# Linear attention and a mixture of adapters on one core: an order given as tables, held stores, warming products, and a pair of batches

## The chip, the cores and the metric

The kernel runs on one core of one Trainium2 chip. TensorE multiplies matrices, VectorE, ScalarE and GpSimd work element by element, SyncE only issues transfers; each takes its instructions in the order in which they were written. The metric is device time in microseconds, from the first instruction to the last landed transfer.

## The reference

Two layers in a row, all in float32. Attention has 8 batches, 8 heads, 576 positions and head size 64; the mixture sees 4608 rows of 512.

```python
phi(x) = concat(relu(x) * cos(pi/2 * pos/S), relu(x) * sin(pi/2 * pos/S))   # 64 -> 128
kv  = einsum('bhsf,bhsd->bhfd', phi(k), v);  z = phi(k).sum(over s)
x   = einsum('bhsf,bhfd->bhsd', phi(q), kv) / (einsum('bhsf,bhf->bhs', phi(q), z) + 1e-6)
x   = x, heads side by side: [8*576, 512]
logits = x @ w_gate                       # 8 experts
top 2 of them, softmax of the two -> w
out = x + sum over the two e of w_e * ((x @ A[e]) @ B[e])      # A[e]: 512 x 16, B[e]: 16 x 512
```

## The kernel before

Positions are split as s = 9p + j, with 64 values of p on partitions and nine of j. GpSimd loads K, V and Q of each batch and turns them into bf16 on the way (`load`, L456): batches 0 and 1 in halves of four heads, the other six whole, 1.18 MB in float32 each. 

For each batch, `relu_k` (L464) takes the positive part of K, `vscale` (L474) multiplies V by the cosine and the sine, and `kv_mm` (L486) sums the products over j, 18 matrix products for four heads, in a PSUM tile `pnd`. `kv_evac` (L498) copies the result into a block matrix `BD`.

Then the 4608 rows go through in 36 groups of 128. A group is (b, x): for x below 4 it has the rows j = x and j = x + 4 of one batch, for x = 4 the rows j = 8 of two batches (`halves`, L542). Its steps: `qt` transposes Q (L556); ScalarE takes the positive part into `qTcs` (L561); VectorE makes the sine half from it with a table of tangents, `TT` (L573); `num` multiplies by BD (L586), 8 products of 128 rows, or 16 of 64 rows where a group has two batches, each with its own BD; `rden` and `xt` (L597, L602) divide by the denominator, which gives 128 rows of x in bf16; `xT` (L610) transposes them in four pieces of 128 columns, and ScalarE or VectorE copies the result out of PSUM (L616 and L618, the two lines of the helper `copy`).

Three groups at a time go through the mixture: `za` (L629) multiplies by `AW`, which holds A and the gate side by side; `max`, `mask`, `sig` and `zg` (L644 to L668) find the top two and weigh; `zgT` (L677) transposes; `dx` adds x (product with the identity, L688) and the adapters' output (product with `Ball`, L690); `osb` copies the sum to an output buffer; `store` (L698), on SyncE, sends it off. The last two of the 13 steps take two groups and one. A store of rows of one batch covers 64 partitions, one of two batches 128. There are three output buffers `OSB`, each for three groups.

A is loaded with d = 4p + i on partition p. Before use, 32 products with a selection matrix `S4` (L425), which GpSimd makes at the start with two instructions (L371, L372), turn A and the gate into pieces of 128 consecutive d.

Nothing of this order is in the loops. Every step is entered in a `Planner` with its engine or a choice of two, a duration, what it needs and makes, and which buffers it uses. `run` (L141) plays the steps through with these durations, takes at each moment the ready step with the smallest entry of the table `PLACES`, gives it the buffer that comes free first, and takes the engine from the table `CHOICE`. The steps are then emitted in the order of their planned starts.

Of the kernel before, what the change touches and what calls it, by code (L numbers as in the profile page):

```python
# [19 lines left out]
LATENCY = {"PE": 0.21, "DVE": 0.13, "ACT": 0.15, "POOL": 0.2, "SP": 0.0}  # L20
DMA_RATE = 0.41e6
DMA_LATENCY = 1.8
DMA_LANES = 8
WINDOW = 0.12


BLOCK, BLOCK_AT, FETCH, FETCH_IDLE = 256, 193, 6.0, 2.5
BEGIN = {"PE": 0.5, "DVE": 0.8, "ACT": 0.7, "POOL": 1.2, "SP": 0.5}

PLACES = [
    -123.82, -97.4, -47.96, -100.66, -30.1, -76.14, 1.18, -17.78, -44.16, -27.45, -102.04, -89.07, -92.75, -20.86,
    8.39, -106.17, -47.52, -51.4, -51.94, -15.2, -20.12, -30.7, -12.73, 41.89, 2.63, 50.86, -32.97, -71.21, -84.2,
    -45.08, -22.7, -44.06, -24.87, -129.18, -56.01, -83.44, -56.45, -23.35, -30.71, -50.56, -9.06, -37.34, -48.99,
    -117.74, 7.85, -46.8, -44.69, -23.35, -67.61, -1.25, -18.65, -42.11, -26.97, -17.26, -8.58, -36.25, -30.45, 61.59,
    31.91, -23.51, 7.81, -59.54, 48.23, -12.48, -11.74, -7.87, -7.7, -66.67, -34.33, -14.61, 22.04, 47.87, -20.83,
    43.94, -35.94, -5.83, 2.99, 18.68, 19.74, 69.59, 65.53, 15.31, -20.71, -7.31, 14.09, -19.09, 24.26, 3.28, 14.51,
    24.35, 40.94, 65.02, 49.01, 82.54, 68.11, 19.64, 70.84, 25.5, 20.21, 19.29, 24.87, 24.94, 64.18, 38.61, 24.78,
    29.61, -12.26, 47.16, 56.95, 48.54, 41.02, 52.02, 49.58, 114.82, 65.11, -7.37, 39.35, 56.79, 16.16, -28.22, 76.43,  # L40
    61.78, 96.28, 70.3, 62.17, 61.7, 83.83, -23.28, 64.9, 39.14, 78.88, 100.53, 74.28, 4.96, 11.73, -67.43, -28.8,
    -34.01, -44.78, -13.42, -65.51, -7.6, 9.03, 21.45, -29.56, -32, -3.44, -20.48, -23.62, -45.49, -61.04, 29, -27.8,
    -17.72, -12.34, 17.18, -5.8, -41.41, -31.76, -12.71, 70.15, -43.08, -85.71, -51.88, 12.95, -31.28, 84.61, -11.54,
    27.95, -15.01, 26.35, 17.38, -4.76, -5.8, -10.36, -29.33, 61.17, 54.51, -2.53, 30.67, 31.34, -9.67, 43.39, 36.24,
    -11.07, 29.89, -28.3, 53.7, 14.2, -22.28, 85.34, 27, 43.28, -14.03, 12.63, -29.88, 26.57, -30.89, 71.13, 64.68,
    -34.05, 41.27, 26.54, 72.12, 38.76, 8.92, 82.64, 17.64, 52.18, 25.58, 1.08, 22.35, -23.14, -66.01, 63.23, 38.57,
    62.14, 23.07, 10.84, 10.98, -23.68, -7.79, 73.89, -37.19, 2.03, -25.04, 19.36, -22.76, 81.5, -23.57, 33.87, 1.89,
    -21.12, -6.03, 19.9, 16.84, -17.44, 14.66, 103.97, 43.62, -33.24, -3.64, -60.62, 62.32, 66.83, 31.16, 68.8, 39.32,
    39.39, 43.79, 52.34, 20.26, 18.55, 38.43, 67.49, 30.64, -19.72, 51.52, -0.52, 31.69, 18.56, 16.08, 32.31, 56.65,
    9.59, 5.09, 40.19, 25.14, 7.76, 72.6, 33.52, 61, 92.58, 20.72, 30.32, 26.33, -1.8, 7.33, 55.26, 53.91, 117.5,  # L50
    26.95, 32.11, 41.24, 51.61, -25.55, 64.34, 16.42, 7.19, 48.57, 34.95, 44.07, 1.01, 10.63, 44.37, 60.54, 12.46,
    32.58, 42.5, 22.25, 15.36, 63.52, 57.28, 20.55, 89.76, 61.89, -35.8, 52.54, 46.1, 40.19, 117.31, 78.88, 59.55,
    29.91, 39.68, 74.62, 33.38, 73.95, 64.93, 68.51, 58.86, 64.3, 79.01, 71.88, 29.75, 26.67, -5.07, 76.92, 9.96,
    72.4, 108.05, 80.33, 48.96, 100.43, -2.47, 62.93, 80.34, 79.57, -21, 59.04, 64.95, 88.66, 65.49, 83.05, 70.43,
    84.07, 57.5, 59.22, 53.56, 45.94, 61.36, 58.67, 64.22, 36.56, 76.22, 57.55, 66.06, 44.35, 117.26, 49.18, 63.07,
    93.92, 69.65, 79.94, 114.34, 45.23, 111.66, 68.79, 75.68, 72.53, 57.81, 47.97, 61.71, 28.28, 120.37, 66.4, 125.69,
    38.58, 91.77, 81.87, 82.14, 65.6, 40.48, 76.56, 78.09, 86.54, 114.37, 85.03, 27.38, 65.38, 40.32, 107.21, 137.42,
    83.89, 101.68, 83.47, 112.71, 91.66, 24.67, 115.02, 58.65, 121.01, 148.52, 55.54, 91.52, 82.4, 48.28, 109.21,
    64.04, 121.31, 47.23, 40.95, 99.89, 55.8, 28.32, 117.95, 23.61, 38.44, 138.24, 97.54, 52.55, 43.2, 16.05, 11.35,
    51.55, 37.09, -47.87, -15.39, -25.41, 28.01, 10.67, -15.69, 21.24, 7.06, -28.41, -20.59, 32.23, -44.3, -16.26,  # L60
    40.19, -16.58, -1.16, -20.84, -50.25, -15.22, -83.33, -46.78, 17.52, -45.48, -54.36, -34, -7.96, -20.96, -86.15,
    7.64, 0.67, 11.92, 77.19, 8.72, 3.46, -51.28, -33.12, -29.65, 50.9, -30.76, -27.31, -30.35, 79.56, -79.28, 8.86,
    -60.44, -52.39, 14.25, -53.52, -13.57, -2.65, -13.97, 21.28, 34.57, 25.69, 21.06, 47.19, 23.41, 20.77, -25.63,
    4.51, 51.34, 53.07, 69.07, 6.72, -12.58, 70.28, 6.9, -1.61, 36.02, 78.96, 63.2, 41.01, 132.03, -27.1, 99.32,
    -1.99, 15.68, 6.14, 20.32, 44.07, 10.98, -102.26, 31.86, 35.53, 75.79, 45.04, 39.6, 25.48, 50.85, 17.07, -16.97,
    9.89, 39.93, 33.37, 42.16, -8.97, -22.49, 32.6, 53.89, 30.65, 3.11, 70.8, 58.34, 21.93, 46.11, 104.63, 23.66,
    -32.61, 6.91, 53.06, -8.51, 73.15, -29.39, 88.37, 41.33, 53, 54.68, 58.28, 133.91, 76.33, 64.59, 23.33, -38.05,
    -14.23, 27.95, 34.17, 54.39, 56.91, 20.35, 63.26, 44.33, 37.33, 23.64, 45.07, 151.11, 93.72, 61.1, 117.26, 35.37,
    25.67, -9.73, 66.86, 97.88, 78.65, 125.31, 70.37, 87.58, 98.38, 66.86, 70.44, 87.69, 62.19, 45.01, 131.73, 8.97,
    56.76, 87.11, 110.15, 82.15, 79.31, 111.79, 87.29, 134.9, 107.5, 137.15, 31.17, 138.15, 46.56, 101.51, 85.3,  # L70
    56.94, 7.46, 25.9, 55.07, 88.7, 73.13, 128.67, 120.65, 47.61, 86.47, 110.69, 69.83, 58.53, 12.4, 93.33, 71.27,
    92.95, 31.16, 85.23, 85.5, 70.42, 95.75, 90.77, 90.1, 124.19, 130.22, 150.77, 134.12, 111.02, 111.53, 155.33,
    117.53,
]
CHOICE = [
    0, 0, 0, 0, 0, 0, 0, 0, 0, 0, 0, 0, 0, 0, 0, 0, 0, 0, 0, 0, 0, 0, 0, 0, 0, 0, 0, 0, 0, 0, 1, 0, 1, 0, 0, 0, 1, 0,
    0, 0, 1, 0, 0, 0, 1, 0, 0, 0, 1, 1, 0, 0, 0, 0, 0, 0, 0, 0, 1, 0, 0, 1, 0, 0, 0, 0, 0, 0, 0, 0, 0, 1, 0, 1, 0, 0,
    0, 0, 0, 0, 0, 0, 0, 0, 0, 0, 1, 0, 0, 0, 1, 0, 0, 0, 0, 1, 0, 0, 0, 0, 0, 0, 0, 0, 0, 0, 0, 0, 0, 0, 0, 0, 0, 0,
    0, 0, 0, 0, 0, 0, 0, 0, 0, 0, 0, 0, 0, 0, 0, 0, 1, 1, 0, 0, 1, 0, 0, 0, 0, 0, 0, 0, 1, 0, 0, 0, 0, 0, 0, 0, 0, 0,
    0, 0, 0, 0, 0, 0, 1, 0, 0, 0, 0, 0, 0, 0, 1, 0, 0, 0, 0, 0, 0, 0, 0, 0, 0, 0, 0, 0, 0, 0, 0, 0, 0, 0, 0, 0, 0, 0,  # L80
    1, 0, 0, 0, 0, 0, 0, 0, 0, 0, 0, 0, 0, 0, 0, 0, 0, 0, 0, 0, 0, 0, 0, 0, 0, 0, 0, 0, 0, 0, 0, 0, 0, 0, 0, 0, 0, 0,
    0, 0, 0, 0, 0, 0, 0, 0, 0, 0, 1, 0, 0, 0, 0, 0, 0, 0, 0, 0, 0, 0, 0, 0, 0, 0, 0, 0, 0, 0, 0, 0, 0, 0, 0, 0, 0, 0,
    0, 0, 0, 0, 0, 0, 0, 0, 0, 0, 0, 0, 0, 0, 0, 0, 0, 0, 0, 0, 0, 0, 0, 0, 0, 0, 0, 0, 1, 0, 0, 0, 0, 0, 0, 0, 0, 0,
    0, 0, 0, 0, 0, 0, 0, 0, 0, 0, 0, 0, 0, 0, 0, 0, 0, 0, 0, 0, 0, 0, 0, 0, 0, 0, 0, 0, 0, 0, 1, 0, 0, 0, 0, 0, 0, 0,
    0, 0, 0, 0, 0, 0, 0, 0, 1, 0, 0, 0, 0, 0, 0, 0, 0, 0, 0, 0, 0, 0, 0, 0, 0, 0, 0, 0, 0, 0, 0, 0, 0, 0, 0, 0, 0, 0,
    0, 0, 0, 0, 0, 0, 0, 0, 0, 0, 0, 0, 0, 0, 0, 0, 0, 0, 1, 0, 0, 0, 0, 0, 0, 0, 1, 0, 0, 0, 0, 0, 0, 0, 1, 0, 0, 0,
    0, 0, 0, 0, 1, 0, 0, 0, 0, 0, 0, 1, 0, 0, 0, 0, 0, 0, 0, 0, 0, 0, 0, 0, 0, 0, 0, 0, 0, 0, 0, 0, 0, 0, 0, 0, 0, 0,
    0, 0, 0, 0, 0, 0, 0, 0, 0, 0, 0, 0, 0, 0, 0, 0, 0, 0, 0, 0, 0, 1, 0, 0, 0, 0, 0, 0, 0, 0, 0, 0, 0, 0, 0, 0, 0, 0,
    0, 0, 0, 0, 0, 0, 0, 0, 0, 0, 0, 0, 0, 0, 0, 0, 0, 0, 0, 0, 0, 1, 0, 0, 0, 0, 0, 0, 0, 0, 0, 1, 0, 0, 0, 0, 0, 0,
    0, 0, 0, 0, 0, 0, 0, 0, 1, 0, 0, 0, 0, 0, 1, 0, 0, 0, 0, 0, 0, 0, 0, 0, 0, 0, 0, 0, 0, 0, 0, 0, 0, 0, 0, 0, 0, 0,  # L90
    0, 0, 0, 0, 0, 0, 0, 0, 0, 0, 0, 0, 0, 0, 0, 0, 0, 0, 0, 0, 0, 0, 0, 0, 0, 0, 0, 0, 0, 0, 0, 0, 0, 0, 0, 1, 0, 0,
    0, 0, 0, 0, 0, 0, 0, 0, 0, 0, 0, 0, 0, 0, 1, 0, 0, 1, 1, 0,
]

class Step:
    def __init__(self, idx, name, alts, due, needs, makes, uses, size, extra, ins):
# [713 lines left out]
```

## Time and profile before

Three runs took 124.2, 124.59 and 124.7 us; the median is 124.59. The profiled execution took 123.85 us, of which its records cover a span of 122.1.

| | busy us | share of the span | instructions |
|---|---|---|---|
| TensorE, products (PE) | 93.8 | 77% | 1328 |
| TensorE, weight loads (PEld) | 69.2 | 57% | 1328 |
| VectorE (DVE) | 98.3 | 81% | 280 |
| ScalarE (ACT) | 77.1 | 63% | 166 |
| GpSimd (POOL) | 28.7 | 24% | 43 |

The busy time of products is modelled: their pipelined ends overlap, so a busy TensorE isn't one at its peak. In the page's second part the span is cut into 40 slices of 3.05 us, and each digit is the busy share of a slice in tenths. In the groups a row reads: line, engine, operation, output <- input with shapes, count, then busy time and the mean of one in ns, then the idle time ahead of them and what ended it.

### The profile page before, as it was taken

How to read it: one execution, taken by the hardware profiler on the slowest of the kernel's cores; microseconds unless marked ns; L12 is line 12 of the kernel's file. 1: busy time of each engine (PE TensorE's matmuls, PEld its weight loads, DVE VectorE, ACT ScalarE, POOL GpSimd, SP SyncE). 2: the span in 40 equal slices, each digit the busy share in tenths (PEclk: the TensorE clock that was granted, in tenths of full speed). 3: DMA queues.
4: the chain of work that ended last, by engine and by line, in shares of the span. 5: the costliest groups of instructions: out<-in, count | busy, mean ns of one | idle time of the engine just before them, and what ended most of it. 6: DMA issues, size and time to landing. Idle time of an engine off the chain costs nothing.

```text
span 122.1 us, 3356 instructions
## 1 busy us (share of the span) xinstructions
PE 93.8 (77%) x1328; PEld 69.2 (57%) x1328; DVE 98.3 (81%) x280; ACT 77.1 (63%) x166; POOL 28.7 (24%) x43
## 2 busy tenths in 40 slices
PE   0007966999579779999799996999999999998100
PEld 0003745888357447877568765867766886662000
DVE  6431649988999999996999999999989999999100
ACT  5659669353693478686785974948194897567200
POOL 6995699922222222202002000000000000000000
PEclk9999996899999999999999999999999999999985
DMA  0999999999999999999999999998827660268791
GB/s 8 162 168 199 205 204 191 209 205 209 207 208 248 295 207 208 244 288 208 232 299 209 293 249 207 207 274 213 194 75 173 173 177 0 90 173 205 263 236 69
DMA packets 17246, 24.06 MB, mean 197 GB/s; under 512 B 2256, under 2 KB 14672, under 8 KB 17232
## 3 DMA queue, kind: packets, MB, share of 16 engines
q0 software_dynamic: 14096, 14.43, 71.2%
q1 hardware_dynamic: 3136, 9.44, 25.8%
q8 instruction: 10, 0.16, 0.5%
q14 instruction: 4, 0.03, 0.1%
HBM read 28.85 MB, written 9.44 MB: 314 GB/s over the span
## 4 chain that ended last, share of the span: by engine, by line
DMA 31%; DVE 28%; PE 24%; issue 5%; ACT 4%; POOL 2%; SPq 0%; DVEq 0%; POOLq 0%; ACTq 0%
DMA Kb<-in_k_dram 27%; PE pnd L492 9%; DVE xt L602 7%; DVE qTcs L573 5%; PE pnd L586 5%; DVE VV L483 4%; DMA out_dram<-osb 4%; PE ps L610 3%; DVE zg L668 2%; DVE BD L506 2%; DVE rden L597 2%; PE ps L629 2%; PE ps L688 2%; PE ps L690 1%; DVE m L644 1%
## 5 line engine op out<-in xcount | busy, mean ns | idle before, releaser
L586 PE MATMUL pnd<-BD,qTcs 128*128 128x130 bf16 (+1 forms) x320 | 23.9, 228 | 3.8 <-DVE xt L602 1.6
L483 DVE TENSOR_TENSOR VV<-Vb,TV 128x2304 bf16<-128x2304 bf16 (+1 forms) x18 | 20.5, 1149 | 6.3 <-DMA Vb<-in_v_dram 6.2
L602 DVE TENSOR_TENSOR xt<-pnd,rden 128x512 bf16<-128x512 f32 x36 | 24.2, 684 | 0.8
L586 PEld LDWEIGHTS <-qTcs 128*128 128x128 bf16 (+1 forms) x320 | 19.4, 103 | 7.7 <-issue 3.1
L561 ACT ACTIVATE qTcs<-ps 128x512 bf16<-128x512 bf16 x36 | 20.1, 601 | 3.1 <-PE ps L556 2.9
L492 PE MATMUL pnd<-VV,KR 64*128 64x260 bf16 x288 | 20.4, 287 | 0.8 <-DVE xt L602 0.5
L616 ACT COPY osb<-ps 128x512 f32<-128x512 f32 (+1 forms) x34 | 18.0, 569 | 4.3 <-DVE osb L618 2.0
L492 PEld LDWEIGHTS <-KR 64*128 64x128 bf16 x288 | 14.3, 99 | 5.1 <-issue 1.3
L616 ACT COPY xT<-ps 128x512 bf16<-128x512 bf16 x24 | 13.9, 588 | 4.8 <-PE ps L610 4.8
L573 DVE TENSOR_TENSOR qTcs<-qTcs,TT 128x512 bf16<-128x512 bf16 x36 | 15.3, 443 | 1.1 <-ACT qTcs L561 0.9
L610 PE MATMUL ps<-ident,xt 128*128 128x128 bf16 x144 | 13.4, 222 | 2.6 <-DVE xt L602 1.5
L690 PE MATMUL ps<-Ball,zgT 128*128 128x512 bf16 x36 | 13.5, 379 | 0.3 <-DVE zgT L618 0.3
L688 PE MATMUL ps<-xt,ident 128*128 128x512 bf16 x36 | 13.6, 379 | 0.0
L610 PEld LDWEIGHTS <-xt 128*128 128x128 bf16 x144 | 9.1, 99 | 6.7 <-DVE xt L602 3.2
L556 PE MATMUL ps<-ident,Qb 128*64 128x128 bf16 x288 | 11.9, 222 | 0.8 <-ACT qTcs L561 0.7
L504 ACT CAST BD<-pnd 64x260 bf16<-64x260 f32 x21 | 7.9, 378 | 5.2 <-PE pnd L492 3.9
L629 PE MATMUL ps<-AW,xT 128*128 128x136 bf16 x144 | 10.8, 223 | 0.4 <-ACT xT L616 0.2
L556 PEld LDWEIGHTS <-Qb 128*64 128x64 bf16 x288 | 8.9, 109 | 3.8 <-issue 2.4
L629 PEld LDWEIGHTS <-xT 128*128 128x128 bf16 x144 | 9.1, 98 | 2.4 <-DVE xT L618 0.6
L661 ACT ACTIVATE sig<-tt 128x24 f32<-128x24 f32 (+2 forms) x13 | 2.9, 222 | 11.2 <-DVE ps L654 6.1
L351 PE MATMUL ps<-tan_d,ones_f 64*128 64x512 f32 (+1 forms) x4 | 2.4, 751 | 9.5 <-DVE tan_d L343 9.5
L459 POOL DMA_DIRECT2D Qb<-in_q_dram x6 | 4.5, 751 | 17.3 <-PE ps L556 10.6
(55 smaller groups left out, 111.1 us busy)
## 6 DMA issues: line engine op xcount, KB each, us to landing
out_dram<-osb SPq DMA_DIRECT2D x20, 256.0 KB, 4.6
Kb<-in_k_dram POOLq DMA_DIRECT2D x6, 576.0 KB, 23.6
Vb<-in_v_dram POOLq DMA_DIRECT2D x6, 576.0 KB, 24.5
Qb<-in_q_dram POOLq DMA_DIRECT2D x6, 576.0 KB, 25.8
out_dram<-osb SPq DMA_DIRECT2D x8, 384.0 KB, 5.2
Kb<-in_k_dram POOLq DMA_DIRECT2D x4, 288.0 KB, 7.5
Vb<-in_v_dram POOLq DMA_DIRECT2D x4, 288.0 KB, 8.5
Qb<-in_q_dram POOLq DMA_DIRECT2D x4, 288.0 KB, 8.9
```

Of the source, the lines that this page charges most:

```text
L483: nc.vector.tensor_tensor(out=o, in0=i, in1=TV[:, cs].unsqueeze(1).to_broadcast([128, n, J, D]), op=ALU.mult)
L492: nc.tensor.matmul(out=pt[:, par, 0:4 * W], lhsT=kt[r, j, 2 * a:2 * a + 2, :].rearrange("p h d -> p (h d)"), rhs=vt[r, 2 * a:2 * a + 2, j, ...
L556: nc.tensor.transpose(out=pt[64 * hh:64 * hh + 64, a, :, x], in_=qt[:, c, j, :], identity=ident)
L561: nc.scalar.activation(tQT[S_(uqt)][:, 0].rearrange("p i x s -> p (i x s)"), pB(up)[:, 0:512], AF.Relu)
L573: nc.vector.tensor_tensor(out=v[1], in0=v[0], in1=f4, op=ALU.mult)
L586: nc.tensor.matmul(out=nd[r, a, 0:4 * W].rearrange("p (h e w) -> p h e w", h=2, e=2)[:, :, par], lhsT=s[:, r], rhs=bd[:, par, a, cs].rearr ...
L602: nc.vector.tensor_tensor(out=tXT[S_(uxt)].rearrange("p (a h d) -> p a h d", a=2, h=4), in0=nd_view(und)[:, :, :, 0:D], in1=tRD[S_(urd)].u ...
L610: nc.tensor.transpose(out=pB(up)[:, c * 128:(c + 1) * 128], in_=tXT[S_(uxt)][:, c * 128:(c + 1) * 128], identity=ident)
L616: nc.scalar.copy(o, i)
L629: nc.tensor.matmul(out=pF(uza)[:, n * AW_W:(n + 1) * AW_W], lhsT=tXTT[S_(u)][:, c, :], rhs=AW[:, c, :], start=(c == 0), stop=(c == 3))
L688: nc.tensor.matmul(out=pF(udx), lhsT=ident, rhs=tXT[S_(uxt)], start=True, stop=False)
L690: nc.tensor.matmul(out=pF(udx), lhsT=tZGT[S_(uzt)][:, i], rhs=Ball, start=False, stop=True)
```

## The change

Six things are done at once.

- **Order, engines and buffers as tables.** The planner's run is gone. `ORDER` lists the 622 steps as they are emitted, `CHOICE` the engine of each, `SLOTS` the buffer of each use. The order, the choices and the buffers differ from those that the planner gave.
- **Stores wait for given loads.** `HOLD` names five stores, each of which waits until a certain load has landed: stores of steps 1, 0, 1, 3 and 4, on the loads of Q of batch 3, K of 3, Q of 4, K of 7 and Q of 7. It is to keep the loads ahead of the stores on the DMA engines. Output buffers go from three to six; `qTcs` from 12 to 8 and `xt` from 20 to 16.
- **Unused products.** A memset makes a tile `warm`; 26 products of it with itself run at the start and 8 more between the two products of the tangent table, whose order is swapped. Their results are used by nothing. They are to keep TensorE's clock up.
- **A used through strided xT.** The selection matrix and its 32 products are gone. A transpose takes, for piece c, the columns d = 4p + c of x, so that A can stay as it was loaded; two plain copies put A and the gate into `AW`.
- **The last two batches paired.** For batches 6 and 7 each of the nine groups has row j of both batches, where before only the one of j = 8 had. Such groups can be stored with neighbours in one transfer over 128 partitions.
- **The loads' order.** It follows from the tables: the first half of batch 1's V ahead of batch 0's second half, and the adapters' weights among the first loads.

```diff
-    pl = Planner()
-    POOLS = {"V": 4, "K": 3, "KR": 3, "Q": 5, "VV": 3, "BD": 4, "QT": 12, "XT": 20, "XTT": 6,
-             "ZG": 2, "ZGT": 2, "OSB": 3, "M8": 2, "W": 2, "RD": 3,
+    pl = Plan()
+    POOLS = {"V": 4, "K": 3, "KR": 3, "Q": 5, "VV": 3, "BD": 4, "QT": 8, "XT": 16, "XTT": 6,
+             "ZG": 2, "ZGT": 2, "OSB": 6, "M8": 2, "W": 2, "RD": 3,
...
+HOLD = [
+    (435, 74), (451, 76), (452, 88), (484, 122), (500, 124),
+]
...
+    def pe_warm(n, up):
+        def f():
+            for _ in range(n):
+                nc.tensor.matmul(out=pF(up), lhsT=warm[:, 0:128], rhs=warm, start=True, stop=True)
+        return f
...
+    pl.add("c", one("DVE", 0.3, c_warm), -99, makes=["warm"])
+    pl.add("warm", one("PE", 7.0, pe_warm(26, ("pS", "w", 0))), -98, needs=["warm"], uses=[("pS", "w", 0)], ins=52)
+    pl.add("warm", one("PE", 1.8, pe_warm(8, ("pS", "w", 1))), -58, needs=[("tan_m", 1)], uses=[("pS", "w", 1)], ins=16)
...
-    def w_turn(up, src, n):
-        def f():
-            for c in range(4):
-                for i in range(4):
-                    nc.tensor.matmul(out=pF(up)[:, c * n:(c + 1) * n], lhsT=S4[:, i, c * 128:(c + 1) * 128],
-                                     rhs=src(i), start=(i == 0), stop=(i == 3))
-        return f
...
+    def w_aw(eng):
+        def f():
+            copy(eng, AW[:, :, 0:ER].rearrange("p i (e r) -> p i e r", e=E), Ald.rearrange("p e i r -> p i e r"))
+            copy(eng, AW[:, :, ER:AW_W], Gld)
+        return f
...
                 nc.tensor.transpose(out=pB(up)[:, c * 128:(c + 1) * 128],
-                                    in_=tXT[S_(uxt)][:, c * 128:(c + 1) * 128], identity=ident)
+                                    in_=tXT[S_(uxt)].rearrange("p (x c) -> p c x", c=4)[:, c], identity=ident)
...
-    seq = [(b, x) for P in range(4) for b in (2 * P, 2 * P + 1) for x in range(4 + b % 2)]
+    seq = []
+    for P in range(4):
+        if P in PAIRED:
+            seq += [("two", 2 * P + 1, j) for j in range(J)]
+        else:
+            seq += [("one", b, x) for b in (2 * P, 2 * P + 1) for x in range(4)] + [("two", 2 * P + 1, 8)]
...
+        hold, issued = dict(HOLD), {}
         for s in order:
-            s.emit()
+            issued[s.idx] = s.emit()
+            if s.idx in hold:
+                tc.add_manual_dep(issued[s.idx].ins, issued[hold[s.idx]].ins.name,
+                                  mybir.DependencyInfo(mybir.DependencyClass.Sync, mybir.DependencyReason.DATA),
+                                  reason="the load goes first")
```

## The prediction

> **What bounds the kernel now.** I read the page's slices first, then busy time by stage, the groups by form, the chain of waits and the end of the timeline.
>
> ```profile
> PE   0007966999579779999799996999999999998100
> ...
> DVE  6431649988999999996999999999989999999100
> ...
> DMA  0999999999999999999999999998827660268791
> ```
>
> The DVE line is nine-tenths busy or more almost everywhere between slice 9 and slice 36, so VectorE is the first suspect; DMA is full to about slice 28 (86 us); PE fills up in the second half. By stage (window; length, then busy us of PE, PEld, DVE, ACT, POOL; clock; DMA; GB/s):
>
> ```profile
> 30.00:40.00 10.00, 7.35 (x121) 5.30 (x115) 9.86 (x22) 6.50 (x13) 2.68 (x4) 1.00 1.20 225
> ...
> 80.00:90.00 10.00, 10.00 (x137) 6.92 (x135) 9.55 (x30) 5.37 (x13) 0.00 (x0) 1.00 0.86 214
> ...
> 110.00:122.00 12.00, 2.96 (x16) 0.98 (x15) 3.12 (x14) 2.90 (x8) 0.00 (x0) 0.83 0.72 197
> ```
>
> In the middle VectorE has 0.14 us of idle in ten and TensorE waits for it; at 80 to 90 both are full. The chain agrees: VectorE pieces from 57 to 76 us, TensorE pieces without a wait from 76 to 90, VectorE to 102, TensorE again to 108. The last 12 us do little arithmetic and wait for stores:
>
> ```profile
> 112.99 0.39 PE L690 MATMUL ps<-Ball,zgT 128*128 128x512 bf16 x1 [0.27 <-DVE zgT L618]
> ...
> 114.46 0.42 DVE L618 COPY osb<-ps 128x256 f32<-128x256 f32 x1 [1.53 <-DMA out_dram<-osb]
> 114.97 0.37 ACT L616 COPY osb<-ps 128x256 f32<-128x256 f32 x1 [1.75 <-DVE osb L618]
> 116.69 0.54 SPq L702 DMA_DIRECT2D out_dram<-osb  x1
> ```
>
> The last product is done at 113.4; its copy waits 1.53 us for an output buffer whose store hasn't landed; the last store, whose data is ready at 115.3, is issued at 116.7 behind ten others that SyncE works off from 106.4 on at 0.47 us or more each, and the span ends at 122.1. From 0 to 83.7 us the two DMA queues (packets, MB, share of 16 engines) read:
>
> ```profile
> q0 software_dynamic: 13892, 14.21, 102.2%
> q1 hardware_dynamic: 1242, 3.91, 12.8%
> ```
>
> Stores (q1) took 12.8% of 83.7 = 10.7 us of DMA time away from the loads, 365 GB/s.
>
> [...] the first 36 kv products (L492) take 3.8 us at 12 to 16 us, later 18 take 1.12; and the clock record shows 0.50 at 19 to 22 us. [...] Every weight load of this trace is packed[...]. [...]
>
> **The change, part by part.**
>
> *Engines.* I counted the instructions of the changed kernel on each engine and took the means of the rows by form. VectorE loses 3 BD copies (0.43 each), 6 xT (0.41), 4 zgT (0.21, 0.28, 2 of 0.35) and one V scaling of 2304 elements (1.35), together 6.3 us; it gains 3 osb copies (0.66), half a K relu (0.47), the memset of `warm` (0.25 to 0.5: the 1056-element one takes 0.50) and two copies for AW (0.6; between 0.4, the 512-element row, and 1.0). The last three fall before 20 us, where VectorE idles 10 us; the osb copies don't. Since neighbours on VectorE overlap by some 0.08 us, the dense stage is relieved of 5.2 - 1.7 = **3.5 us**. ScalarE gains 6.2 us (6 xT of 0.59, 3 BD of 0.38, 4 zgT, a V scaling in nine pieces of about 0.41; less 3 osb, a relu of 1.16 and the two AW casts). It idles 45 of 122 us, so nothing in the sum, but its queue is strict: behind the nine pieces (3.7 us) stand the q evacuations that VectorE's tan products wait for.
>
> *A through strided xT.* The 32 selection products (L425) lay on the chain from 23.95 to 25.35 us: -1.4 us on TensorE there. GpSimd's two S4 instructions (3.7 us) go; the loads behind them were queued anyway: 0. The 144 weight loads of xt (L610) become strided. A load takes 98 ns, and four transposes occupy 0.22 to 0.38 us. Low end: no change. High end: half speed, 98 ns more on each, none hidden: 14.1 us of TensorE. I take 0.
>
> *Pairing batches 6 and 7.* Eight groups have 16 products of 64 rows instead of 8 of 128: 0.57 against 0.47 us on the chain, +0.8 us of TensorE at the end. All nine groups of the pair now need batch 7's keys. After batch 7's K relu VectorE has 24.0 us of work (25.7 before), TensorE 23.6, so nothing starves so long as that relu isn't late. It ran at 85.5, K having landed at 83.65.
>
> *Holds.* SyncE issues in order, so a store that waits for a load blocks all behind it; nobody but the reuse of output buffers waits for those. Eight stores, 1.97 MB, stand ahead of the one that waits for batch 7's K load. At 365 GB/s they cost 5.4 instead of 10.7 us: K lands at 78.4. VectorE isn't there yet, so this buys only its waits for data: 1.1 us at 57 (relu on a K load). With six output buffers for three, stores held to about 82 us return before their buffers are due (TensorE reaches the first such group after batch 7's kv). The other 7.5 MB need 20 us at 365 GB/s, 28 at 270: done by 110 at worst.
>
> *Tail.* The last nine groups are stored by 4 instructions over 128 partitions instead of 9, eight of them over 64, and the output buffer is free. From the last product: 113.4 + 0.5 copy + 0.45 issue + 5.4 landing (as now) = 119.7 instead of 122.1: **-2.4 us**.
>
> *Warm products.* 26 of 512 columns from about 3 us: eight at 0.43 us (half clock), the rest at 0.215 (the spacing of the dx products): over at 10.3. Then a tan product (0.4 to 0.5), eight more (1.7), and the big tan product (1.0 to 2.1): kv may start at 13.4 to 14.5 instead of 12.2, but takes 1.1 us per half instead of 1.9. The second half of V lands a transfer (1.5 us) later, as batch 1's is put ahead, so kv ends near 16.6 instead of 16.0; the first num products then run at full clock and save about 1 us. I book 0, between -1.5 and +1.5.
>
> **Sum.** VectorE 3.5, of which I count 2.5, as TensorE is as full from 76 us on and gets 0.8 more; VectorE's waits, 0.9 us at 20 to 30 (TensorE cold and busy with selection) and 1.1 at 57, of which I count 1.0; tail 2.4: 5.9 us. 124.6 - 5.9 = **118.7 us**.
>
> **The rivals.**
> A, the strided weight load is slow. TensorE idles 7.5 of the 90 us from 20 to 110; 14.1 us more leave 6.6 on the path: 124.6 + 6.6 - 2.4 (tail) - 1.4 (selection) = 127.4, slower. For it: no packed load tells; TensorE is co-bound. Against: L610 is pipelined, 55 to 95 ns a transpose, so part of a slower load hides.
> B, the order gives the VectorE gain back: its queue waits for ScalarE (nine pieces) or for batch 7, and only the tail is left: 124.6 - 2.4 = 122.2. For it: three engines wait for one another in strict order. Against: ScalarE's idle 45 us.
> C, everything counts: 3.5 + 2.0 + 2.4 + 0.5 at the start = 8.4: 116.2. For it: loads come 5 us earlier; against: TensorE's full stretch from 76 to 90.
>
> **How the numbers follow.** Forecast 0.56, C 0.12, B 0.17, A 0.15 (mild forms of it near 125 included). The range leaves A's slow end and the tips out: 115.3 to 123.9. Faster: 0.56 + 0.12 + 0.15 of B = 0.83. Within 0.5%: 0.02 of B and 0.03 of A. Slower: 0.12 of A.
>
> **What would show it.** VectorE busy near 95.6 us (98.3 now), ScalarE near 83; xt weight loads still near 98 ns and four transposes in 0.22 to 0.4 us (A: about twice); the K relu of batch 7 at 83 or so and its load landed near 78; the last osb copy without a DMA wait and the last store issued within 1 us of it; kv at 62 ns a product from the first. I am wrong if VectorE's idle between 20 and 110 us (4.8 now) grows by more than 3 us, or if the end still waits for a queue of stores.

## The result, and the profile after

| | us, median (lowest to highest) | ratio to before, 95% interval |
|---|---|---|
| before | 124.55 (124.2 to 124.7) | |
| forecast | 118.7, range 115.3 to 123.9 | |
| changed | 117.53 (116.29 to 118.66) | 0.941 [0.933, 0.948] |
| changed, beside the first four experiments | 116.98 (116.09 to 117.49) | 0.939 [0.936, 0.942] |

The change saves about 7 us. The records of the profiled execution cover a span of 115.4 us, 6.7 less than before. The slices of the changed kernel's page, 2.89 us each:

```profile
PE   0999957679669999999999998979999999998600
...
DVE  6823479979799999999999999999998999998700
...
DMA  0999999999999999999999999999384298989991
```

TensorE is now busy from the first slices on, which are the unused products. VectorE is full, with small gaps, from slice 12 to slice 36 (about 32 to 104 us), nearly as before. The full stretch of DMA ends at slice 28, now 81 us instead of 86. Two of the stages, in the columns of the prediction:

```profile
30.00:40.00 10.00, 7.98 (x120) 5.89 (x122) 9.79 (x26) 7.85 (x16) 2.22 (x3) 1.00 1.21 208
80.00:90.00 10.00, 9.89 (x175) 7.32 (x173) 9.46 (x27) 7.07 (x16) 0.00 (x0) 1.00 0.53 139
```

From 30 to 40 us VectorE's idle is as small as it was (0.21 us in ten), but ScalarE does 7.85 us of work for 6.50. From 80 to 90 TensorE gets 175 products done where it did 137, of another mix, in about the same busy time, so that figure alone doesn't say that TensorE is full. After 110 us no engine computes any more. The end, from the timeline of the changed kernel (start, duration, instruction, and in brackets the idle time ahead and what ended it; SPq rows are issues by SyncE, here five):

```profile
108.62 0.39 PE L604 MATMUL ps<-Ball,zgT 128*128 128x512 bf16 x1 [0.36 <-ACT zgT L242]
...
109.05 0.42 DVE L244 COPY osb<-ps 128x256 f32<-128x256 f32 x1 [0.31 <-PE ps L604]
...
109.51 0.37 ACT L242 COPY osb<-ps 128x256 f32<-128x256 f32 x1 [0.94 <-DVE osb L244]
...
103.99 6.26 SPq L618 DMA_DIRECT2D out_dram<-osb  x5
```

The last copy waits for its product and no longer for a store. The last store is issued as soon as its data is there (the five issues end at 110.25), and 5.2 us later the span ends. From the last product's end, 109.0, to the end it is 6.4 us; before, it was 122.1 - 113.4 = 8.7.

One landmark splits the gain: VectorE's K relu of batch 7 starts at 82.20 us instead of 85.51. So 3.3 us come before it and 3.4 after it. Of these the end has 2.3; the other 1.1 lie between the relu and the last product's end, 26.8 us instead of 27.9.

### The profile page after: what moved, and what is told of

Read it like the earlier page. It is cut to its first block, busy times and chain, and to the rows that moved or that the text cites. A ratio compares the mean times of both kernels' runs of the same rounds, so it can differ in the third digit from the quotient of the medians.

```text
span 115.4 us, 3462 instructions
## 1 busy us (share of the span) xinstructions
PE 96.9 (84%) x1383; PEld 68.8 (60%) x1394; DVE 95.6 (83%) x273; ACT 83.0 (72%) x182; POOL 25.7 (22%) x41
## 4 chain that ended last, share of the span: by engine, by line
PE 43%; DVE 21%; DMA 14%; ACT 9%; issue 5%; POOL 3%; POOLq 0%; ACTq 0%; DVEq 0%
DMA Kb<-in_k_dram 14%; PE pnd L506 10%; PE pnd L412 10%; PE ps L530 5%; PE ps L476 5%; PE ps L602 4%; DVE xt L522 4%; DVE VV L403 4%; PE ps L543 4%; DVE qTcs L493 3%; PE ps L604 3%; ACT qTcs L481 3%; PE ps L591 2%; DVE zg L582 2%; ACT osb L242 2%
## 5 line engine op out<-in xcount | busy, mean ns | idle before, releaser
L522 DVE TENSOR_TENSOR xt<-pnd,rden 128x512 bf16<-128x512 f32 x36 | 24.3, 687 | 0.8
L506 PE MATMUL pnd<-BD,qTcs 128*128 128x130 bf16 (+1 forms) x384 | 22.5, 223 | 2.9 <-DVE xt L522 2.4
L403 DVE TENSOR_TENSOR VV<-Vb,TV 128x2304 bf16<-128x2304 bf16 (+1 forms) x17 | 19.1, 1135 | 4.0 <-DMA Vb<-in_v_dram 4.0
L506 PEld LDWEIGHTS <-qTcs 128*128 128x128 bf16 (+1 forms) x384 | 18.0, 103 | 6.2 <-issue 3.7
L242 ACT COPY xT<-ps 128x512 bf16<-128x512 bf16 x30 | 17.1, 587 | 2.3 <-PE ps L530 1.9
L242 ACT COPY osb<-ps 128x512 f32<-128x512 f32 (+1 forms) x31 | 16.4, 574 | 1.9 <-DVE osb L244 0.9
L493 DVE TENSOR_TENSOR qTcs<-qTcs,TT 128x512 bf16<-128x512 bf16 x36 | 14.0, 409 | 1.3 <-ACT qTcs L481 0.7
L297 PE MATMUL ps<-warm 128*128 128x512 bf16 x34 | 9.2, 435 | 3.1 <-DVE warm L291 3.1
L401 ACT ACTIVATE VV<-Vb,TVf 128x128 bf16<-128x128 bf16 (+1 forms) x27 | 9.2, 433 | 3.5 <-DMA Vb<-in_v_dram 3.5
L604 PE MATMUL ps<-Ball,zgT 128*128 128x512 bf16 x26 | 9.7, 379 | 0.4 <-ACT zgT L242 0.4
L297 PEld LDWEIGHTS <-warm 128*128 128x128 bf16 x34 | 3.6, 109 | 7.9 <-DVE warm L291 3.1
```

The lines of the kernel that those rows point to most:

```text
L242: nc.scalar.copy(o, i)
L403: nc.vector.tensor_tensor(out=o, in0=i, in1=TV[:, cs].unsqueeze(1).to_broadcast([128, n, J, D]), op=ALU.mult)
L493: nc.vector.tensor_tensor(out=v[1], in0=v[0], in1=f4, op=ALU.mult)
L506: nc.tensor.matmul(out=nd[r, a, 0:4 * W].rearrange("p (h e w) -> p h e w", h=2, e=2)[:, :, par], lhsT=s[:, r], rhs=bd[:, par, a, cs].rearr ...
L522: nc.vector.tensor_tensor(out=tXT[S_(uxt)].rearrange("p (a h d) -> p a h d", a=2, h=4), in0=nd_view(und)[:, :, :, 0:D], in1=tRD[S_(urd)].u ...
L604: nc.tensor.matmul(out=pF(udx), lhsT=tZGT[S_(uzt)][:, i], rhs=Ball, start=False, stop=True)
```

## The experiments

Numbers in steps such as 173 are indices in the tables `ORDER` and `CHOICE`. All comparisons are with the kernel before on the same chip; its medians there were 124.38, 124.45 and 124.46 us. The changed kernel itself ran beside the first four experiments only.

### The changed kernel again

> The changed kernel once more, as the measure for the runs beside it. Every theory: 117.5 us, between 116.3 and 118.7; VectorE busy 95.6 us, the K relu of batch 7 near 82.2.

Measured: 116.98 us, 0.939 [0.936, 0.942]; span 115.1, the K relu of batch 7 at 82.13. The reference for what follows is 117.0 to 117.5 us.

### Without the holds

```diff
-HOLD = [
-    (435, 74), (451, 76), (452, 88), (484, 122), (500, 124),
-]
+HOLD = []
```

> The changed kernel without the five waits of stores on loads; all else as it is. Theory (holds only move loads ahead; VectorE sets the time of batch 7's K relu, now 82.2 us): K of batch 7 lands some 4 us later, near 85, so the relu waits 2 to 3 us and the end moves by 1 to 2.5: 118.5 to 120. Rival 1 (holds do nothing, as TensorE and VectorE are behind the loads anyway): 117.5. Rival 2 (held stores pile up at the end): 116 to 117, with the last store landing sooner after its issue than the 5.4 us of now.

Measured: 117.27 us, 0.941 [0.939, 0.944]. The stores' DMA queue from 0 to 83.7 us (packets, MB, share of 16 engines), first of the changed kernel, then without holds:

```profile
q1 hardware_dynamic: 784, 2.36, 8.0%
```

```profile
q1 hardware_dynamic: 784, 2.36, 8.1%
```

The stores did move away from the loads: 2.36 MB of them in this stretch instead of 3.91. But the same stores move without the holds, and the first one goes out at 43.6 us instead of 43.3 (35.1 in the kernel before). The load of K of batch 7 shows it too: issued at 54.2 us, it lands 24.3 us later, at 78.5; without the holds it is issued at 54.3 and takes 24.3 us as well. In the kernel before it took 28.1 us from 54.9 on. So the holds do nothing that these runs show. The stores go later for another part of the change; that it is the place which the new order gives to the products and copies ahead of a store is likely, but no run shows it alone.

### Without the unused products

```diff
-    pl.add("warm", one("PE", 7.0, pe_warm(26, ("pS", "w", 0))), ...
-    pl.add("warm", one("PE", 1.8, pe_warm(8, ("pS", "w", 1))), ...
+    pl.add("warm", one("PE", 7.0, pe_warm(0, ("pS", "w", 0))), ...
+    pl.add("warm", one("PE", 1.8, pe_warm(0, ("pS", "w", 1))), ...
```

> The changed kernel without the 34 unused products (the memset of their tile stays). Theory (booked at 0, between -1.5 and +1.5): kv of batch 0 starts sooner, at 11 to 12 us instead of 12.6, but runs at 106 ns a product instead of about 64, and the first num products run at half clock near 20 us; the first xt is at 20.3 us plus or minus 1 and the whole at 116.5 to 118.5. Rival (the warm clock is what makes the start of the changed kernel): the first xt 1.5 to 3 us later, the whole 119 to 120.5.

Measured: 119.22 us, 0.956 [0.953, 0.960]: 2.2 us slower than with them. TensorE's timeline, first of the changed kernel, then without the unused products:

```profile
15.91 1.19 PE L412 MATMUL pnd<-VV,KR 64*128 64x260 bf16 x18 [1.19 <-DVE VV L403]
17.03 1.08 PE L476 MATMUL ps<-ident,Qb 128*64 128x128 bf16 x32
```

```profile
15.96 2.13 PE L412 MATMUL pnd<-VV,KR 64*128 64x260 bf16 x18 [1.80 <-DVE VV L403]
18.03 1.92 PE L476 MATMUL ps<-ident,Qb 128*64 128x128 bf16 x32
```

Both start the second half of batch 0's kv at 15.9, when V is scaled. In the second, 18 products take 2.13 instead of 1.19 us and the 32 transposes 1.92 instead of 1.08. VectorE's first `xt` comes at 21.97 instead of 20.30. Not all of these 1.67 us last: at the K relu of batch 7 the lag is 0.97 (83.17 instead of 82.20). A second delay comes at 91 us, where an output copy of VectorE waits 1.18 us:

```profile
91.07 0.69 DVE L244 COPY osb<-ps 128x512 f32<-128x512 f32 x1 [1.18 <-PE pnd L506]
```

From there on the lag is 2.25, up to the last output copy at 111.30 instead of 109.05. The record names a product; a store issued at 84.8 us lands at 90.8, so it may have been an output buffer. At the end only 0.8 us of it is left (spans of 116.2 and 115.4), since the last stores land sooner after their copies. The traced execution, 118.18 us, was also the fastest of the six. So the worth of 2.2 us is that of the medians; the trace shows where about 1 us of it arises, and not how the rest does in the other executions. The forecast had this at zero.

### The unused products in the kernel before

```diff
+        nc.vector.memset(warm, 1.0)
         nc.vector.memset(halfpi, math.pi / 2.0)
...
+            for _ in range(8 if i else 26):
+                nc.tensor.matmul(out=pF(("pS", "t", i)), lhsT=warm[:, 0:128], rhs=warm, start=True, stop=True)
             nc.tensor.matmul(out=pF(("pS", "t", i))[:, 0:hi - lo], lhsT=ones_f,
```

> The kernel before with a warm tile, 26 unused products ahead of the first product of the tangent table and 8 ahead of the second, nothing else changed. In the changed kernel the same products were worth 2.2 us (117.0 against 119.2). Theory (the gain is the half clock of the first 36 kv products, the transposes and the first num products, and VectorE behind them starts its dense stretch earlier): faster by 1.5 to 2.2 us, 122.2 to 122.9, with kv at 62 ns a product and the first xt of VectorE about 1.5 us earlier. Rival (in this kernel the second half of V or the selection products hold the first xt, so the clock buys nothing): within 0.5 of 124.4 us. The forecast's booking of zero would give the same.

Measured: 124.66 us, 1.0013 [0.9995, 1.0031]. The same products that are worth 2.2 us in the changed kernel are worth nothing here. They work (18 kv products in 1.19 us), yet VectorE's first `xt` is at 20.68 instead of 20.48. The rival was right that something else holds it, though it named the wrong thing. The timeline of this kernel from 17 us:

```profile
17.11 2.02 POOL L376 TENSOR_SCALAR_AFFINE_SELECT S<-S 128x2048 bf16<-128x2048 bf16 x1
17.27 2.47 DVE L487 TENSOR_TENSOR VV<-Vb,TV 128x1152 bf16<-128x1152 bf16 x1
...
19.66 0.75 DVE L577 TENSOR_TENSOR qTcs<-qTcs,TT 128x512 bf16<-128x512 bf16 x2
...
20.13 0.62 PE L590 MATMUL pnd<-BD,qTcs 128*128 128x130 bf16 x4 [2.08 <-DVE qTcs L577]
```

The value scaling takes 2.47 us; its like takes 0.75. It ends 0.6 us after GpSimd's instruction on the selection matrix, which ends at 19.13; behind it waits the tangent product, and behind that TensorE, 2.08 us. The kernel before shows the same:

```profile
16.68 1.91 POOL L372 TENSOR_SCALAR_AFFINE_SELECT S<-S 128x2048 bf16<-128x2048 bf16 x1
...
17.39 1.48 DVE L573 TENSOR_TENSOR qTcs<-qTcs,TT 128x512 bf16<-128x512 bf16 x1 [0.93 <-ACT qTcs L561]
```

A tangent product that takes 0.41 elsewhere takes 1.48 us, while GpSimd works on the selection matrix until 18.59.

In both traces the stretched instruction starts while GpSimd's is under way. In this kernel the tangent product that starts at 16.93, ahead of GpSimd's instruction (17.11), takes 0.43 us, and the scaling that starts after it, at 17.27, is stretched past GpSimd's end. GpSimd's instruction takes 2.02 us instead of the 1.91 of the kernel before, 0.11 more where it overlaps with that tangent product by 0.25, so it is hardly held up itself. Why VectorE's instruction is held, no run here shows.

More follows. Behind TensorE's wait the clock record has a mean of 0.68 from 20 to 30 us (0.88 in the kernel before, where it reads 0.50 from 19 to 22), and 18 kv products of batch 1 take 2.13 us instead of 1.19:

```profile
23.25 2.13 PE L496 MATMUL pnd<-VV,KR 64*128 64x260 bf16 x18
```

VectorE's fourth `xt` is then 1.65 us later than in the kernel before. There was also less to win. The kernel before has its first 36 kv products in one stretch of 3.8 us, and behind them the transposes already run fast, where they take 1.92 us in the changed kernel without unused products:

```profile
15.91 1.08 PE L556 MATMUL ps<-ident,Qb 128*64 128x128 bf16 x32
```

The changed kernel has no selection matrix. That its removal is what lets the warm products count is argued from these traces; no run took the selection matrix away alone, and the transposes say that it can't be all.

### The transposes on packed columns

The products with A then use a wrong row order; only the time is of interest.

```diff
-                                    in_=tXT[S_(uxt)].rearrange("p (x c) -> p c x", c=4)[:, c], identity=ident)
+                                    in_=tXT[S_(uxt)][:, c * 128:(c + 1) * 128], identity=ident)
```

> The changed kernel with packed transposes: piece c takes the columns 128c to 128c+127 again, while A stays as it was loaded, so the adapters' part is computed with rows of A that don't belong to the columns of x. It shows the cost of the step of four alone. The changed kernel's weight loads of xt take 113 ns, 98 before. Theory (the loads are pipelined beside products, so 15 ns more are hidden): loads back at 98 ns, total 117.5, less than 0.5 us better. Rival (each costs its 15 ns on a full TensorE: 144 x 0.015 = 2.2 us): 115.3 to 116.5.

Measured: 117.06 us, 0.940 [0.937, 0.943], the same. The weight loads of `xt` (lowest, median and highest ns), first of the changed kernel, then packed:

```profile
L530 PEld LDWEIGHTS <-xt x144: 111/113/135, 21.4 to 104.3; 128*128 128x128 bf16 x144
```

```profile
L530 PEld LDWEIGHTS <-xt x144: 95/98/99, 21.7 to 104.1; 128*128 128x128 bf16 x144
```

With a step of four bf16 values the median load takes 15 ns longer, 2.2 us in 144, all of it beside other work.

### The old engines on the new order

Written compactly; in the changed kernel the first line's steps have 0 and the second line's 1.

```diff
+for i in (173, 181, 189, 229, 253, 293, 73, 85, 97, 428, 460, 491, 524): CHOICE[i] = 1
+for i in (480, 482, 562): CHOICE[i] = 0
+CHOICE[115] = 0    # 1 in the changed kernel: the scaling on ScalarE
```

> The changed kernel with its engine choices as the kernel before had them in the moved places: six xT copies, three masked copies of the key-value sums, four zgT copies and one value scaling return from ScalarE to VectorE, three output copies return from VectorE to ScalarE; order, pairing and warm products stay. VectorE gets about 3.5 us more to do, all but one copy of it before 109 us. Theory (VectorE is the engine that sets the pace from 30 to 110 us, TensorE close behind): slower than the changed kernel by 2.5, to about 119.7 us, with the last batch's K relu and the last output copy both later. If VectorE alone bounds: by 3.5, 120.7 us. Rival (TensorE, 9.9 busy of 10 in the window 80 to 90 us of the changed kernel, is now the bound, and the engine choice is worth nothing): within 0.5 of 117.2 us.

Measured: 123.48 us, 0.993 [0.990, 0.995]: 6.2 us slower than with the new engines, more than either figure. By the K relu of batch 7, at 88.4 us, it is 6.2 behind, so the rest of the kernel loses nothing more. The first two of the moved copies show how it goes. VectorE's timeline, first of the changed kernel, then with the old engines:

```profile
31.51 0.20 DVE L517 RECIPROCAL rden<-pnd 128x8 f32<-128x8 f32 x1
31.62 2.58 DVE L403 TENSOR_TENSOR VV<-Vb,TV 128x2304 bf16<-128x2304 bf16 x2
34.11 0.20 DVE L517 RECIPROCAL rden<-pnd 128x8 f32<-128x8 f32 x1
```

```profile
31.66 0.20 DVE L517 RECIPROCAL rden<-pnd 128x8 f32<-128x8 f32 x1
31.84 0.42 DVE L244 COPY xT<-ps 128x512 bf16<-128x512 bf16 x1
32.19 1.35 DVE L403 TENSOR_TENSOR VV<-Vb,TV 128x2304 bf16<-128x2304 bf16 x1
33.45 0.42 DVE L244 COPY xT<-ps 128x512 bf16<-128x512 bf16 x1
33.79 1.35 DVE L403 TENSOR_TENSOR VV<-Vb,TV 128x2304 bf16<-128x2304 bf16 x1
35.05 0.20 DVE L517 RECIPROCAL rden<-pnd 128x8 f32<-128x8 f32 x1
```

The lag grows from 0.15 to 0.94 us, 0.40 for each copy of 0.42, and it is never made up. All in all VectorE has before that relu six xT (2.5), three BD (1.3), four zgT (1.4) and one scaling (1.35) more and two output copies (1.4) less: 5.2 us. With 1.1 us of new waits (0.99 for a transpose at 61.8, 0.15 for ScalarE at 72) this is 6.3, and the lag grew by 6.1.

### VectorE's load alone

```diff
             issued[s.idx] = s.emit()
+            if s.idx in (173, 181, 189, 229, 253, 293, 73, 85, 97):
+                nc.vector.memset(junk, 1.0)
```

> The changed kernel with nine unused memsets of 1024 bf16 values on VectorE, put behind the six xT copies and three BD copies that were moved to ScalarE: some 0.49 us each (from the memset of 1056 bf16 values, 0.50 us), 4.4 us together, as much as VectorE had more in the kernel with the old engines. Nothing waits for them and they wait for nothing but their turn. That kernel was 6.2 us slower. Theory (VectorE's load accounts for 4.4 of these 6.2 us, the other 1.8 being the order that no longer fits the engines): slower by 4.0 to 4.6 us, 121.2 to 121.8. Rival 1 (TensorE is as tight, and only part of VectorE's load counts, as forecast 2.5 of 3.5): by 3.1 us, 120.3. Rival 2 (misfit is most of it, load alone matters little): by less than 2 us, under 119.2.

Measured: 126.79 us, 1.016 [1.010, 1.022]: 9.3 to 9.8 us slower than the changed kernel, twice what the theory said. The memsets were mis-sized:

```profile
L706 DVE MEMSET junk<- x9: 912/912/912, 32.3 to 79.4; 128x1024 bf16 x9
```

The row that I had read, 528 uint32 in 0.50 us, is of as many bytes but half as many elements. By elements the rows agree: 0.89 ns a value here, 0.94 there, and 0.94 for the 512 values of `warm` in the changed kernel, 0.48 us. Nine times 0.91 are 8.2 us, and each memset also has 0.16 us of idle ahead of it, ended by nothing that the trace shows. In the timelines of the old engines above, VectorE's instructions begin 0.07 to 0.09 us before the one ahead has ended; these don't. One `xt` behind the last of the nine tells the rest, of the changed kernel and of this one:

```profile
71.64 0.69 DVE L522 TENSOR_TENSOR xt<-pnd,rden 128x512 bf16<-128x512 f32 x1
```

```profile
80.79 0.69 DVE L523 TENSOR_TENSOR xt<-pnd,rden 128x512 bf16<-128x512 f32 x1
```

It is 9.15 us later, 0.44 of that from before the first memset (the granted clock was 0.83 from 20 to 30 us in this run). The nine memsets thus cost 8.7 us, 0.97 each, and the lag is still 9.1 at the end (the spans are 124.5 and 115.4). Nothing was absorbed. With the load of the old engines, which counted as fully, both rivals fall for load that is added: TensorE takes no part of it off the path between 30 and 80 us, and misfit of the order is not most of it.

### Still less on VectorE

```diff
+for i in (277, 301, 341, 480): CHOICE[i] = 0    # 1 in the changed kernel
```

> The changed kernel with four more copies moved from VectorE to ScalarE: three xT copies (about 55, 64 and 73 us) and one output copy (about 53 us). VectorE loses 1.9 us, ScalarE, 83 us busy of 115, gains 2.4. If VectorE alone bounds: faster by 1.9 us, 115.3. If VectorE and TensorE bound together: faster by 0 to 0.7, 116.5 to 117.2. Rival (ScalarE's queue is now so full that q evacuations come late): slower by 0.5 to 2 us, 117.7 to 119.2.

Measured: 119.57 us, 0.962 [0.957, 0.966]: slower by 2.0 to 2.6, as the rival said. VectorE has less to do and waits. ScalarE's timeline of this kernel, then TensorE's and VectorE's:

```profile
72.66 3.70 ACT L401 ACTIVATE VV<-Vb,TVf 128x256 bf16<-128x256 bf16 x9
76.25 0.59 ACT L242 COPY xT<-ps 128x512 bf16<-128x512 bf16 x1
76.71 0.61 ACT L242 COPY osb<-ps 128x512 f32<-128x512 f32 x1
```

```profile
76.89 0.41 PE L543 MATMUL ps<-AW,xT 128*128 128x136 bf16 x4 [2.14 <-ACT xT L242]
```

```profile
77.41 0.32 DVE L558 MAX8 m<-ps 128x8 f32<-128x8 f32 x3 [2.22 <-ACT osb L242]
```

One of the moved xT copies, step 301, starts on VectorE at 73.51 in the changed kernel. It now stands behind the nine pieces of the value scaling in ScalarE's queue and starts at 76.25; the mixture's products wait 2.14 us for it and VectorE's maximum 2.22 (its record names the output copy behind the xT copy). In the changed kernel the work behind those nine pieces is two output copies, for which nobody waits soon. (The four copies are made at 57, 63, 73.5 and 85 us in the changed kernel; the expectation had all four too early.) The first two bring no loss and little gain: 1.1 us less on VectorE put it ahead by only 0.2 us at 66. TensorE is busy for all of the 7 us from 60 to 67 there, and VectorE waits 0.28 us for it. So here what is added to VectorE counts in full, but what is still taken off soon meets TensorE.

### The new engines on the old order

Written compactly.

```diff
+ENGINES = {150: 1, 158: 0, 166: 0, 66: 1, 429: 0, 73: 0, 71: 0, 90: 0, 190: 0, ...}    # 32 steps
         for s in order:
+            s.choose(ENGINES.get(s.idx, CHOICE[s.idx]))
             s.emit()
```

> The kernel before, its order of emission kept, with the engines of the changed kernel for 32 copies, evacuations, scalings and K relus from the second batch on (where a step exists in both). VectorE has about 5.3 us less to do (6 xT, 4 BD, 3 zgT, one scaling less, 2 output copies more), ScalarE as much more. Theory (VectorE's load alone sets the pace): faster by 3.7 to 5.3 us, 119.1 to 120.7. Rival (engines and order must fit each other; on the old order ScalarE's queue gives it back, as the old engines lost more than their load on the new order): faster by less than 2 us or slower, 122.4 to 127.

Measured: 128.77 us, 1.035 [1.031, 1.039]: 4.3 us slower than before, though VectorE is busy for 95.2 us instead of 98.3. ScalarE's queue of this kernel, and TensorE's and VectorE's, at two places:

```profile
29.70 2.13 ACT L476 ACTIVATE KR<-Kb 128x2304 bf16<-128x2304 bf16 x1
31.72 0.21 ACT L668 ACTIVATE sig<-tt 128x24 f32<-128x24 f32 x1
...
72.58 3.71 ACT L488 ACTIVATE VV<-Vb,TVf 128x256 bf16<-128x256 bf16 x9
76.17 0.61 ACT L568 ACTIVATE qTcs<-ps 128x512 bf16<-128x512 bf16 x1
```

```profile
76.83 0.38 PE L695 MATMUL ps<-xt,ident 128*128 128x512 bf16 x1 [2.53 <-ACT qTcs L568]
```

```profile
31.97 0.18 DVE L674 TENSOR_TENSOR w<-ps,sig 128x24 f32<-128x24 f32 x1 [1.55 <-ACT sig L668]
...
77.93 0.21 DVE L604 RECIPROCAL rden<-pnd 128x8 f32<-128x8 f32 x1 [2.37 <-PE pnd L593]
```

On the old order a K relu of 2.13 us stands ahead of a sigmoid for which VectorE waits, and the nine pieces ahead of a q evacuation for which TensorE and then VectorE wait. VectorE's two waits alone are 3.9 us. So the relief of VectorE is bought with long instructions on ScalarE (2.13 and 3.71 us in these rows), and here it pays only where the order puts something behind them that can wait.

### The last two batches unpaired

```diff
-    PAIRED = (3,)
+    PAIRED = ()
```

`ORDER` and `CHOICE` are renumbered, with the added stores put behind those that they come from.

> The changed kernel with the last two batches' groups made one batch at a time as in the kernel before, so that their stores have 64 partitions again and there are five more of them; engines of the copies and order otherwise kept. Theory (pairing costs 0.8 us of TensorE's weight loads and products and takes away 1.5 to 2.4 us of the end, which before waited for the queue of stores): slower than the changed kernel by 0.7 to 1.6 us, 117.9 to 118.8, the last product's end about as before and the time from it to the end back from 6.4 toward 8.7 us. Rival (pairing only adds TensorE work, the end is short because of the order of the stores): faster by 0.8, 116.4 us, with the end still 6.4 us.

Measured: 119.56 us, 0.962 [0.959, 0.964]: 2.0 to 2.6 us slower. The last copies on VectorE and the last issues on SyncE:

```profile
108.94 0.42 DVE L244 COPY osb<-ps 128x256 f32<-128x256 f32 x1 [0.31 <-PE ps L604]
```

```profile
104.53 7.73 SPq L621 DMA_DIRECT2D out_dram<-osb  x8
112.35 0.94 SPq L618 DMA_DIRECT2D out_dram<-osb  x1
```

The last copy is within 0.11 us of the changed kernel's. Pairing therefore cost nothing that reached the path, against the 0.8 us booked. Nor is TensorE busier for it: 97.7 us in 1394 products with the pairs (the changed kernel again), 98.3 in 1330 without. But the last store is issued at 112.35, 2.6 us after its data is ready (ScalarE's half ends at 109.77).

### Paired, but stored in halves

```diff
             if kind == "two":
                 o = out[(b - 1) * S:(b + 1) * S].rearrange("(p j) d -> p j d", j=J)[:, x:x + n]
+                if b == 7:
+                    for r in (0, 64):
+                        d = nc.sync.dma_start(out=o[r:r + 64], in_=tOSB[S_(uo)][r:r + 64, i:i + n])
+                    return d
```

> The changed kernel, paired as it is, but each store of the last two batches' pair groups issued as two of 64 partitions. The same bytes, seven or so issues of some 0.6 to 1.2 us more on SyncE in the last 20 us. Theory (the number of issues on SyncE is what made the end of the kernel before long): the end grows by one issue at least (0.6 to 1.2 us), and by up to 2 if the last stores queue up: 117.8 to 119.2 us. Rival (the end is the store's landing time and the wait for an output buffer, not the issues): within 0.4 of 117.2 us.

Measured: 119.56 us, 0.962 [0.958, 0.967], as much as unpaired, with the last copy at the same moment (108.97):

```profile
104.40 9.36 SPq L620 DMA_DIRECT2D out_dram<-osb  x8
```

The same bytes leave in eight issues, almost without a pause from 104.40 on, the last one ending at 113.76. Its data was ready at 109.80. So the whole gain of the pairing is that SyncE has fewer issues, each over 128 partitions; splitting changes both, and this run can't tell them apart. The eight issues take 0.6 to 1.6 us each, the last two of the changed kernel 0.3; why, no run shows.

### A spare output buffer in the kernel before

```diff
-    tOSB = sb([128, 3, DM], FP32, "osb", POOLS["OSB"])
+    tOSB = sb([128, 3, DM], FP32, "osb", POOLS["OSB"] + 1)
...
+    pl.slot[("OSB", 12)] = 3
```

> The kernel before with a fourth output buffer which the last group alone uses, so that its output copy waits for no store; nothing else changed. In the kernel before the last output copy waited 1.53 us for a store to read its buffer out. Theory (the end waits for SyncE's queue of stores, and the buffer wait is a symptom of it): the copy comes earlier, the stores do not, and the gain is 0 to 0.6 us: 123.9 to 124.5. Rival (the wait for the buffer sets the end): faster by 1.5 us, 123.0.

Measured: 124.47 us, 1.0004 [0.999, 1.002]. VectorE's last copy and the last issues:

```profile
113.86 0.42 DVE L618 COPY osb<-ps 128x256 f32<-128x256 f32 x1 [0.48 <-PE ps L690]
```

```profile
106.87 10.09 SPq L705 DMA_DIRECT2D out_dram<-osb  x10
117.05 0.59 SPq L702 DMA_DIRECT2D out_dram<-osb  x1
```

The copy no longer waits for a buffer and is done 0.6 us earlier, but the store still waits for its turn on SyncE. The wait of 1.53 us in the chain of the kernel before was a symptom of the queue.

## Why the prediction was right, and where its steps were not

The time was 1.2 us below the forecast, inside the range. It was reached by steps of which several were off in opposite directions, so part of the closeness is luck.

- **VectorE sets the pace: right. Its relief of 3.5 us, of which 2.5 were counted: too small.** VectorE was busy 95.6 us and ScalarE 83.0, as forecast, and VectorE's idle from 20 to 110 us grew by 1.3 us, not by the 3 that would have spoken against it. The cut to 2.5 rested on TensorE's busy figure from 76 us on. The old engines put back cost 6.2 us, the added memsets their whole time, so up to 80 us TensorE took nothing off; behind that no run tested it. The other way round TensorE is close, as the kernel with still less on VectorE shows. The working also took off three output copies where only two lie before 82 us.
- **VectorE's waits, 2.0 us of which 1.0 were counted: half of that came.** By the stages, the wait for K at 57 us is gone (VectorE idles 0.35 us from 50 to 60 instead of 1.59), but from 20 to 30 us it idles 1.63 us instead of 0.91.
- **Rival B, the nine pieces in ScalarE's strict queue: the mechanism is real.** It is what happened in the new engines on the old order (+4.3 us) and with still less on VectorE (+2.1 to 2.6). The order keeps the changed kernel clear of it. So there is no gain "of the engines" apart from the order: with them on the old order there is a loss.
- **Unused products, booked at zero within 1.5: mis-sized.** They are worth 2.2 us by the medians. How many would run slow was an estimate; in the changed kernel the first eight start 0.43 us apart (3.13 to 6.09 us) and the other 18 about 0.22, and the last ends at 10.46, where 10.3 was forecast. The forecast's other half was also there: kv of batch 0 ends at 17.1 instead of 16.0, since V comes later. Together the first `xt` is at 20.30 instead of 20.48, which is why the sum near zero did no harm; that the two offset each other is luck.
- **Selection matrix on GpSimd, booked at zero: the step that was missing.** I asked which loads were queued behind it, not which VectorE instruction runs beside it. In two traces one that did took 1.1 and 1.7 us longer than its like.
- **Strided loads at zero: right**, with 113 ns instead of 98, hidden. Rival A is out; its doubled load was an estimate that no trace had shown. (The idle of TensorE that it counted, 7.5 us, is 7.7 by the stages; that changes nothing.)
- **Holds: the effect was there, the cause was not.** K of batch 7 was forecast to land at 78.4 and lands at 78.5, but at 78.6 without the holds too. The figure fits so well by luck: K's landing in the kernel before, taken as 83.65, was at 83.05. The expected consequence, a relu of batch 7 that doesn't wait and starts at about 83, came at 82.2.
- **Tail -2.4: measured -2.3**, for one of the two stated reasons: the fewer stores. The free output buffer alone was worth nothing. **Pairing +0.8 on TensorE: measured zero.**

The parts don't add up. Taken from the changed kernel one at a time, engines, unused products and pairing cost 6.2, 2.2 and 2.3 us, 10.7 together, while the whole change gives 7. With the old engines all the rest of the change saves 1.0 us (123.48 against 124.45), less than the end alone. Added to the kernel before, the engines cost 4.3 us and the unused products give nothing. The new order itself, with the old engines, was not tried without the other parts, so its own share stays open. No version tried beats the changed kernel: without holds and with packed columns it is the same within the intervals.

## What to carry to other kernels

Where one engine is busy without gaps, count what is moved onto or off it in full, idle between instructions included (here nine memsets of 0.91 us cost 0.97 each), and don't discount it for another engine whose busy figure is as high: see whether that one gets more done in the same busy time. Taking off more stops paying where the next engine is close behind, as here with 0.2 us for 1.1. What is moved to a queue in strict order costs what stands behind it (here TensorE waited 2.53 us behind nine pieces of 3.71), so look for the first instruction behind a long one and for who waits for it. At an end that waits for stores, count the issues on the issuing engine before bytes or buffers: here the same bytes in more issues, of 64 partitions each, took 2.0 to 2.6 us more, and a spare buffer gave nothing.

## What the runs showed of the hardware that was not expected

- TensorE's clock record reads 1.00 from 9 to 30 us in the kernel without unused products, while 18 products take 2.13 us there at 12.03 and 15.96 and 1.19 at 24.72. In the kernel before with unused products 18 of them take 2.13 us at 23.25, where the record does show a lower clock (a mean of 0.68 from 20 to 30 us). So at the start of these runs the duration of like products tells more than the record.
- 1.4 us of idle on TensorE end at 21.04 us in the changed kernel and at 20.89 in the one with memsets, the same program up to 32 us. From 20 to 30 us the clock record has a mean of 1.00 in the first and of 0.83 in the second, and eight products with `BD` take 0.63 us in the first (at 21.95) and 1.09 in the second (at 22.42).
- The V scaling took 2.47 us on VectorE, and its like 0.75, while GpSimd worked on the selection matrix (2.02 us); the trace books it as busy time, not as a wait.
- A weight load with a step of four bf16 values takes 113 ns, packed 98 (medians of 144).
- A memset of 1024 bf16 ones took 912 ns, one of 528 uint32 498, one of 512 bf16 ones 480: the time goes with the elements, not with the bytes.
